# A recurrence and a mixer on one core: another order of the instructions, and transposes as pairs of 64-row blocks

## The chip, the core and the metric

The kernel runs on one core of a Trainium2 chip. A core has a tensor engine (TensorE, PE in the profile; its weight loads are listed as PEld), three engines for elementwise work (VectorE or DVE, ScalarE or ACT, GpSimd or POOL) and a queue engine (SyncE or SP) that issues transfers; sixteen DMA engines carry these. Each engine works through its own list of instructions in order and waits on semaphores for the others. The metric is the device time of one execution in microseconds (us).

## What is computed

Two stages follow each other, and the result is that of the second. The first is a recurrence over 768 time steps for 4 batches and 8 heads of 40 channels, with a state of 40x40 for each head:

```python
for t in range(S):
    y[:, :, t] = np.einsum('bhd,bhde->bhe', rt, state)
    Sa = np.einsum('bhde,bhe->bhd', state, at)
    state_decay = state * wt[:, :, None, :] - np.einsum('bhd,bhe->bhde', Sa, bt)
    state = state_decay + np.einsum('bhd,bhe->bhde', vt, kt)
```

The second takes y as x, with the 8 heads side by side as 320 channels:

```python
theta = x @ w_theta
yr = np.einsum('ts,bsd->btd', w_tok_r, x * np.cos(theta))
yi = np.einsum('ts,bsd->btd', w_tok_i, x * np.sin(theta))
u = x + (yr + yi)
return u + np.maximum(u @ w_ch, 0.0)
```

Inputs and output are float32; the kernel multiplies in bfloat16.

## The kernel before

The recurrence is worked off in 24 chunks of 128 time steps, 6 for each batch (`N = 24`, index `i`). For each chunk these steps follow; the names in quotes are the kinds by which the code calls its operations:

- Loads of w, k, b, a, v and r, 160 KB each, issued by SyncE (`load`, L409 and L421). The buffers are few (4 for w, 4 for k and b, 5 for a, 2 pairs for r), so a load waits until its buffer is free.
- Preparation (`prep`, L438 on): logarithm and cumulative sums of w (ACT and PE, "cs"), exponentials (ACT), products of k, b and a with them (POOL, L429: "kb", "ah"), casts of v and r (POOL or ACT, L435 and L434).
- Transposes on PE (`transpose_pairs`, L391; `turn_runs`, L538; `turn_back`, L557). A transpose is a matmul with the identity: the block of 128x128 is the stationary operand, the identity the moving one, and the result stands in PSUM, the accumulator memory of 8 banks. ACT (L394) or DVE (L397) then evacuates it to SBUF. "tkb" has 8 blocks, "ta", "tv" and "nut" 4 each, "tr" 8, "to" 8, "tb" 4.
- Scores (`scores`, L569): for the eight heads, eight matmuls of 64 rows and 128 columns ("spsi", "sphi", "slv", "slu"). Two heads lie in the upper and lower half of the rows and write to two different banks. A triangular mask follows, on DVE in one step (L578), or on ACT as a copy (L580) with a selection on POOL behind it (L582).
- The recurrence between chunks ("x0", "nu", "gt", "gd", L610 to L684) and the read-out ("y", L793 to L809).
- The mixer: x transposed ("xt", L711, 5 blocks for two chunks), times w_theta ("th", L763 and L773), copied (L828, "eth"), sine and cosine on ACT, products with x on POOL (L865, "z"); once a batch is complete, the mix over tokens ("row", L881: two times six matmuls of 320 columns for each output block), u transposed ("ut", L711), times w_ch ("ch", L763, L773), and the result stored (L920). The token weights come in through POOL's own queue (L960, "wdma") and are transposed ("wt", L968, 6 blocks).

All these operations are first collected in a list of 1602 with costs and dependences (`Plan.add`). Nothing is ordered at run time: `ORDER` (L26) is a written list of the 1602 numbers in which the operations are emitted, so it fixes the order on every engine. `HOMES` (L122) names the PSUM bank of each new PSUM tile in that order, and `PICK` (L138) names the operations that take the second of their two forms, such as a mask on ACT instead of DVE. PSUM is divided: banks 0 to 3 hold tiles of two banks (`doubles`, L355: only scores, and the token mix of the last two blocks), banks 4 to 7 tiles of one (`singles`, L356). Eleven transposes (`CROSSBAR`, L24) don't run on PE but as DMA transposes from SyncE's queue. `WARM` (L145) puts 49 matmuls on constant data into the start.

Of the kernel before, what the change touches and what calls it, by code (L numbers as in the profile page):

```python
# [144 lines left out]
WARM = {21: 25, 30: 4, 33: 1, 28: 8, 41: 11}  # L145


class Op:
# [53 lines left out]
def mm(n):  # L202
    return max(n / 2.4 + 2.5, 25.0)
# [853 lines left out]
```

## Time and profile before

| what | value |
|---|---|
| times of three runs | 197.72, 198.29 and 202.19 us; median 198.29 |
| span of the profiled execution | 197.8 us |
| instructions | 8019 |
| matmuls | 3288 |
| first input load issued | 0.8 us |
| last input load issued | 150.8 us |
| data moved | 32.75 MB, mean 166 GB/s |

The span runs from the first to the last instruction of the profiled execution; it stands 0.5 us under the median. An engine is busy from the start of an instruction to its end. Matmuls overlap each other, so PE's busy time says only when PE had something under way, and the distance between the starts of two matmuls says what one costs. In the rows of groups, "out<-in" names the tiles, the numbers behind the bar are the sum in us and the mean in ns, and the last part is idle time of the engine before these instructions with what ended it. SPq is SyncE's queue: the time that issuing a transfer took. The granted clock of TensorE is 1.00 in all stages.

### The profile page before, as it was taken

How to read it: one execution, taken by the hardware profiler on the slowest of the kernel's cores; microseconds unless marked ns; L12 is line 12 of the kernel's file. 1: busy time of each engine (PE TensorE's matmuls, PEld its weight loads, DVE VectorE, ACT ScalarE, POOL GpSimd, SP SyncE). 2: the span in 40 equal slices, each digit the busy share in tenths (PEclk: the TensorE clock that was granted, in tenths of full speed). 3: DMA queues.
4: the chain of work that ended last, by engine and by line, in shares of the span. 5: the costliest groups of instructions: out<-in, count | busy, mean ns of one | idle time of the engine just before them, and what ended most of it. 6: DMA issues, size and time to landing. Idle time of an engine off the chain costs nothing.

```text
span 197.8 us, 8019 instructions
## 1 busy us (share of the span) xinstructions
PE 187.6 (95%) x3288; PEld 150.3 (76%) x3288; DVE 164.3 (83%) x261; ACT 151.7 (77%) x337; POOL 145.1 (73%) x210
## 2 busy tenths in 40 slices
PE   7888999999989999999999999999999999999992
PEld 6776787777768788878878888888887878767661
DVE  5269899999989999888887988999999988675453
ACT  3584979799889988979988598888998986575111
POOL 8267544679879999699799939769699697558100
PEclk9999999999999999999999999999999999999999
DMA  6999879989999999999998899988998274863055
GB/s 119 210 212 163 154 161 196 182 166 197 233 174 173 207 171 185 190 185 223 153 210 168 153 187 170 188 148 169 182 155 163 43 177 102 87 194 104 0 191 174
DMA packets 134644, 32.75 MB, mean 166 GB/s; under 512 B 124816, under 2 KB 134608, under 8 KB 134608
## 3 DMA queue, kind: packets, MB, share of 16 engines
q1 hardware_dynamic: 131680, 29.19, 75.1%
q0 software_dynamic: 2784, 2.97, 9.6%
q8 instruction: 25, 0.41, 0.9%
q10 hardware_dynamic: 144, 0.08, 0.1%
q14 instruction: 11, 0.09, 0.1%
HBM read 29.54 MB, written 3.93 MB: 169 GB/s over the span
## 4 chain that ended last, share of the span: by engine, by line
PE 68%; DMA 9%; ACT 8%; SPq 6%; DVE 3%; issue 3%; POOL 1%; ACTq 0%; DVEq 0%; POOLq 0%
PE ps_s L881 17%; PE ps_s L391 10%; PE ps_d L569 9%; PE ps_s L763 5%; SPq L409 4%; DMA raw_w<-in_w_dram 3%; DMA raw_kb<-in_k_dram 3%; PE ps_s L711 3%; PE ps_s L652 2%; PE ps_s L629 2%; SPq L421 2%; DMA raw_r<-in_r_dram 2%; PE ps_s L538 2%; PE ps_s L773 2%; ACT cs L850 2%
## 5 line engine op out<-in xcount | busy, mean ns | idle before, releaser
L429 POOL TENSOR_TENSOR kb<-raw_kb,ex 128x320 bf16<-128x320 f32 x46 | 36.8, 811 | 9.7 <-DMA raw_kb<-in_k_dram 3.3
L881 PE MATMUL ps_s<-zr,wtok_r 128*128 128x320 bf16 x132 | 37.6, 299 | 0.0
L881 PE MATMUL ps_s<-zi,wtok_i 128*128 128x320 bf16 x132 | 37.5, 299 | 0.0
L578 DVE TENSOR_TENSOR lamu<-ps_d,mask_p 128x1024 bf16<-128x1024 f32 x22 | 26.8, 1219 | 1.7 <-PE ps_d L569 1.6
L578 DVE TENSOR_TENSOR psi<-ps_d,mask_p 128x1024 bf16<-128x1024 f32 x22 | 26.8, 1218 | 1.6 <-PE ps_d L569 1.4
L578 DVE TENSOR_TENSOR lamv<-ps_d,mask_p 128x1024 bf16<-128x1024 f32 x17 | 20.7, 1218 | 2.6 <-PE ps_d L569 1.8
L429 POOL TENSOR_TENSOR ah<-raw_a,we 128x320 bf16<-128x320 f32 x22 | 19.0, 866 | 3.6 <-DMA raw_a<-in_a_dram 1.6
L578 DVE TENSOR_TENSOR phi<-ps_d,mask_n 128x1024 bf16<-128x1024 f32 x17 | 20.7, 1218 | 0.9 <-PE ps_d L569 0.8
L865 POOL TENSOR_TENSOR zi<-cs,xp 128x320 bf16<-128x320 f32 x21 | 16.9, 816 | 3.3 <-ACT cs L850 3.3
L881 PEld LDWEIGHTS <-wtok_r 128*128 128x128 bf16 x144 | 14.0, 97 | 4.5
L569 PE MATMUL ps_d<-aT,kbT 64*128 64x128 bf16 x384 | 17.1, 217 | 0.2
L881 PEld LDWEIGHTS <-wtok_i 128*128 128x128 bf16 x144 | 14.1, 98 | 3.5
L391 PE MATMUL ps_s<-wide,kb 128*128 128x128 bf16 x184 | 15.0, 223 | 1.0 <-POOL kb L429 0.7
L865 POOL TENSOR_TENSOR zr<-cs,xp 128x320 bf16<-128x320 f32 x19 | 15.3, 810 | 0.7 <-ACT cs L850 0.7
L667 POOL TENSOR_TENSOR gt<-sum,ex 128x320 bf16<-128x320 f32 x13 | 9.5, 733 | 8.0 <-DVE sum L663 4.8
L800 PE MATMUL ps_s<-kb,lamv 128*128 128x40 bf16 x192 | 15.0, 180 | 0.0
L802 PE MATMUL ps_s<-kb,lamu 128*128 128x40 bf16 x192 | 14.9, 179 | 0.0
L569 PEld LDWEIGHTS <-kbT 64*128 64x128 bf16 x384 | 11.8, 94 | 3.1 <-ACT kbT L394 1.0
L800 PEld LDWEIGHTS <-lamv 128*128 128x128 bf16 x192 | 13.2, 96 | 0.6
L887 DVE TENSOR_TENSOR up<-ps_s,xp 128x320 bf16<-128x320 f32 x22 | 10.7, 488 | 3.5 <-PE ps_s L881 3.1
L435 POOL CAST r<-raw_r 128x640 bf16<-128x640 f32 x12 | 8.6, 720 | 6.5 <-DMA raw_r<-in_r_dram 6.5
L445 ACT ACTIVATE lw<-raw_w 128x320 bf16<-128x320 f32 x24 | 11.4, 475 | 2.6 <-DMA raw_w<-in_w_dram 2.6
(176 smaller groups left out, 606.7 us busy)
## 6 DMA issues: line engine op xcount, KB each, us to landing
raw_w<-in_w_dram SPq DMA_DIRECT2D x24, 160.0 KB, 4.1
raw_v<-in_v_dram SPq DMA_DIRECT2D x24, 160.0 KB, 3.9
raw_a<-in_a_dram SPq DMA_DIRECT2D x24, 160.0 KB, 4.2
raw_kb<-in_k_dram SPq DMA_DIRECT2D x24, 160.0 KB, 3.7
raw_kb<-in_b_dram SPq DMA_DIRECT2D x24, 160.0 KB, 4.0
raw_r<-in_r_dram SPq DMA_DIRECT2D x24, 160.0 KB, 4.4
out_dram<-oo SPq DMA_DIRECT2D x9, 160.0 KB, 2.0
wrow_i<-in_moe_w_tok_i_dram POOLq DMA_DIRECT2D x6, 192.0 KB, 5.3
```

The lines of the kernel that those rows point to most:

```text
L391: nc.tensor.transpose(out=dst[:, c:c + 128], in_=pair(src, g), identity=ident)
L429: pool = ("POOL", lambda: nc.gpsimd.tensor_tensor(out=dst, in0=in0, in1=in1, op=ALU.mult))
L445: add("ACT", "ln", i, lambda: nc.scalar.activation(out=paired(lw)[:, :, :, 0:D], in_=paired(raw_w[s4]), func=AF.Ln), 473, [("raw_w", s4)], ...
L569: nc.tensor.matmul(t[:, q, g, :], lhsT=lhs[g][rows(q)], rhs=rhs[g][rows(q)], start=True, stop=True)
L578: add("DVE", kindm, i, lambda: nc.vector.tensor_tensor(out=flat, in0=whole(), in1=mask.to_broadcast([128, 2 * G, 128]), op=ALU.mult), 1217 ...
L667: add("POOL", "wgt", i, lambda: nc.gpsimd.tensor_tensor(out=new_state, in0=sum_t, in1=wm.to_broadcast([128, 8, D]), op=ALU.mult), 830, [(" ...
L763: nc.tensor.matmul(ps(pk)[:, 0:DM], lhsT=lhs[:, 3 * c + kt, :], rhs=wt[:, 3 * c + kt, :], start=kt == 0, stop=kt == 2, skip_group_check=n ...
L800: nc.tensor.matmul(o, lhsT=lamv[:, p, g, :], rhs=kb[:, 0, h, 0:D], start=first, stop=False, skip_group_check=True)
L802: nc.tensor.matmul(o, lhsT=lamu[:, p, g, :], rhs=kb[:, 1, h, 0:D], start=False, stop=True, skip_group_check=True)
L865: pool = ("POOL", lambda: nc.gpsimd.tensor_tensor(out=dst, in0=in0, in1=in1, op=ALU.mult))
L881: nc.tensor.matmul(acc(), lhsT=wtok[nm][j][:, s], rhs=zs[c][:, s], start=n == 0 and c == 0, stop=n == NT - 1 and c == 1)
L887: add("DVE", "uadd", q, lambda: nc.vector.tensor_tensor(out=u, in0=acc(), in1=x, op=ALU.add), 488, [pk, x_key(q)], [u_key(q)], at="row")
```

## The change

The 1602 operations, their dependences and the inputs stay. Seven things change.

1. `ORDER` is another permutation. Up to about the first fifth the order on each engine is as before (the first 91 of PE's 596 operations, 70 of ACT's, 38 of DVE's, 24 of POOL's, 47 of SyncE's 180); behind that every engine has another order.
2. A transposing operation has a second form. In place of one matmul of 128 rows and 128 columns for a block it issues two of 64 rows and 64 columns, the upper half of the rows into one bank and the lower half into the next.
3. `PICK` names the operations in their other form: 94 before, 177 now. 54 of them are transposing operations that become pairs: 13 "tkb", 12 "nut", 8 "ut", 6 "tr", 5 "tv", 4 "xt", 4 "wt", 2 "ta". Together they have 308 of the 749 blocks that PE transposes (in 139 operations).
4. The evacuations read a pair's result from two banks (`src[:, :, ...]`), with the halves of 64 interleaved in the destination.
5. PSUM is one tile of eight banks, and any bank may hold any tile; a tile of two banks takes any two neighbours.
6. Some work moves between engines, by the other entries of `PICK`: masks on ACT and POOL 23 instead of 18 of 96; "eth" copies on DVE 9 instead of 1; evacuations "ea" on DVE 10 instead of 8, "ekb" 6 instead of 8, "enut" 5 instead of 7; "egd" copies on DVE 2 instead of 0, "nx" 4 instead of 2; casts of v on ACT 7 instead of 5, of r 3 instead of 0; products "z" on DVE 1 of the usual ones instead of 5, "kb" 2 more and "ah" 1 more on DVE.
7. `WARM`'s matmuls go to named banks 0 to 2 instead of the bank of the operation that they precede.

The list was planned with at most five of SyncE's transfers under way. The code holds nothing of this but the order.

Counted in the order of PE's operations, neighbours change between 128-row and 64-row work (scores, pairs, and the 64-row parts of "th" and "ch") 134 times before and 164 times now:

| up to PE's operation | stands at, before | changes before | changes now | blocks in pairs now |
|---|---|---|---|---|
| 142 | about 60 us | 48 | 49 | 33 |
| 441 | about 150 us | 107 | 133 | 248 |
| 596 | the end | 134 | 164 | 308 |

SyncE's transfers 48 to 56 are, before: r6, r6, b8, r8, w9, k8, r8, a8, w10 (the letter is the tensor, the number the chunk, r in two halves). Now: r8, r6, k8, r6, v10, b8, w9, r8, a8. The four token weight loads that POOL issues between 45.0 and 49.2 us are spread: counted by PE's work ahead of them, of which 26 us correspond to about 39 us of time and 42 to about 60, they stood together at 33 to 35 us and stand now at 26, 34, 39 and 39.

The diff, cut to its core (the lists are left out):

```diff
-PICK = [
+PICK = {
...
-WARM = {21: 25, 30: 4, 33: 1, 28: 8, 41: 11}
+WARM = {21: (0, 25), 30: (1, 4), 33: (2, 1), 28: (1, 8), 41: (1, 11)}
...
-        for n in PICK:
-            self.ops[n].eng, self.ops[n].fn = self.ops[n].alts[0]
+        for n, m in PICK.items():
+            o = self.ops[n]
+            o.eng, o.fn = o.alts[m - 1][:2]
+            if o.eng == "PE":
+                o.new = (o.new[0], 2)
...
-    doubles = [psum.tile([128, 2, 512], FP32, name=f"ps_d{i}") for i in range(DOUBLE // 2)]
-    singles = [psum.tile([128, 512], FP32, name=f"ps_s{i}") for i in range(BANKS - DOUBLE)]
+    banks = psum.tile([128, BANKS, 512], FP32, name="banks")
...
-        return doubles[h[0] // 2] if len(h) == 2 else singles[h[0] - DOUBLE]
+        return banks[:, h[0]:h[0] + 2] if len(h) == 2 else banks[:, h[0]]
+
+    def split(key):
+        return len(plan.home[key]) == 2
...
-    def transpose_pairs(dst, srcs):
-        for j, src in enumerate(srcs):
-            for g in range(G):
-                c = (j * G + g) * 128
-                nc.tensor.transpose(out=dst[:, c:c + 128], in_=pair(src, g), identity=ident)
...
+    def turned(kind, i, key, srcs, reads, cost, at="tile"):
+
+        def go():
+            if not split(key):
+                t = ps(key).bitcast(BF16)
+                for m, src in enumerate(srcs()):
+                    nc.tensor.transpose(out=t[:, m * 128:m * 128 + 128], in_=src, identity=ident)
+                return
+            for m, src in enumerate(srcs()):
+                for c in range(2):
+                    nc.tensor.transpose(out=ps(key)[:, c].bitcast(BF16)[:, m * 64:m * 64 + 64],
+                                        in_=src[rows(c)], identity=ident[rows(c), rows(c)])
+        add("PE", kind, i, go, cost, reads, [key], at=at, new=(key, 1), tail=tail(128),
+            alts=(("PE", go),))
...
+        def copy(op, out, dt, w):
+            one, src = n * w // 64, ps(psk) if w == 32 else ps(psk).bitcast(BF16)
+            if not split(psk):
+                at = (part or 0) * one
+                op(out=out, in_=src[:, at:at + one])
+            elif part is not None:
+                op(out=out, in_=src[:, part, 0:one])
+            else:
+                op(out=out.rearrange("p (n c w) -> p c n w", c=2, w=w),
+                   in_=src[:, :, 0:one // 2].rearrange("p c (n w) -> p c n w", w=w))
...
-            t = ps(o.new[0])
-            t = t[:, 0] if len(t.shape) == 3 else t
-            for _ in range(WARM[o.idx]):
-                nc.tensor.matmul(t[:, 0:128], lhsT=busy[:, 0:128], rhs=busy[:, 0:128],
+            at, n = WARM[o.idx]
+            for _ in range(n):
+                nc.tensor.matmul(banks[:, at, 0:128], lhsT=busy[:, 0:128], rhs=busy[:, 0:128],
                                  start=True, stop=True, skip_group_check=True)
```

More of the change, by code (lines that the diff above doesn't have):

```diff
@@ L508, in tr @@
             n = 4 * len(srcs)
[L509 to L510 removed]
+            turned(kind, i, p, lambda: pairs_of(srcs), skeys, n * mm(128))
             evac(eng, kinde, i, p, dst, n * 128, writes=[dkey])
@@ L531, in turn_runs, with tokens @@
         pr = ("ps", "t" + nm, i)
+        def tokens(t, q):
+            if nm == "r":
+                return t.rearrange("p (a t q g) -> p q t a g", a=2, q=8, g=2)[:, q]
+            return t.rearrange("p (t q g) -> p q t g", q=8, g=G)[:, q]
         def go():
[L534 removed]
             for q in range(8):
[L536 to L540 removed]
+                src = t[:, q].rearrange("p c d -> p (c d)")
+                if not split(pr):
+                    nc.tensor.transpose(out=tokens(ps(pr).bitcast(BF16), q), in_=src, identity=ident)
+                    continue
+                for c in range(2):
+                    nc.tensor.transpose(out=tokens(ps(pr)[:, c].bitcast(BF16)[:, 0:512], q),
+                                        in_=src[rows(c)], identity=ident[rows(c), rows(c)])
+        add("PE", "t" + nm, i, go, 8 * mm(128), [(nm, s)], [pr], new=(pr, 1), tail=tail(128),
+            alts=(("PE", go),))
         for x, (dst, dkey) in enumerate(dsts):
@@ L706, in feature_major @@
         n = len(blocks)
-        def go():
-            t = ps(p).bitcast(BF16)
-            for m, src in enumerate(blocks):
-                nc.tensor.transpose(out=t[:, m * 128:m * 128 + 128], in_=src, identity=ident)
-        add("PE", kind, q, go, n * mm(128), skeys, [p], at=at, new=(p, 1), tail=tail(128))
+        turned(kind, q, p, lambda: blocks, skeys, n * mm(128), at)
         evac("ACT", kinde, q, p, dst[:, 0:n, :].rearrange("p a b -> p (a b)"), n * 128,
@@ L963, in wtok_block @@
             p = ("ps", "wt" + nm, tb)
-            def go(row=row, p=p):
-                t = ps(p).bitcast(BF16)
-                for s in range(NT):
-                    nc.tensor.transpose(out=t[:, s * 128:(s + 1) * 128],
-                                        in_=row[:, s * 128:(s + 1) * 128], identity=ident)
-            add("PE", "wt", i, go, 6 * mm(128), [("wrow", nm, tb % 2)], [p], new=(p, 1),
-                tail=tail(128))
-            dst = wtok[nm][tb]
-            add("DVE", "ewt", i, lambda dst=dst, p=p: nc.vector.tensor_copy(
-                out=dst, in_=ps(p)[:, 0:384].bitcast(BF16).rearrange("p (a b) -> p a b", b=128)),
-                550, [p], [("wtok", nm, tb)], alts=(("ACT", lambda dst=dst, p=p: nc.scalar.copy(
-                    out=dst.bitcast(FP32),
-                    in_=ps(p)[:, 0:384].rearrange("p (a b) -> p a b", b=64))),))
+            turned("wt", i, p, lambda row=row: [row[:, s * 128:(s + 1) * 128] for s in range(NT)],
+                   [("wrow", nm, tb % 2)], 6 * mm(128))
+            evac("DVE", "ewt", i, p, wtok[nm][tb].rearrange("p a b -> p (a b)"), 768,
+                 [("wtok", nm, tb)])
     def mix_rows(bi):
```

44 lines of the change are left out of this document (15 added, 29 removed), and 242 rows, old and new, of tables (HOMES, ORDER, PICK).

## The prediction, made before the changed kernel ran

> **What bounds the kernel now.** I read the page's busy times and chain first, then the table by stage, then single matmuls in the timeline, and last the transfers of the stage before 60 us.
>
> ```profile
> span 197.8 us, 8019 instructions
> PE 187.6 (95%) x3288; PEld 150.3 (76%) x3288; DVE 164.3 (83%) x261; ACT 151.7 (77%) x337; POOL 145.1 (73%) x210
> ...
> q1 hardware_dynamic: 131680, 29.19, 75.1%
> q0 software_dynamic: 2784, 2.97, 9.6%
> ...
> PE 68%; DMA 9%; ACT 8%; SPq 6%; DVE 3%; issue 3%; POOL 1%; ACTq 0%; DVEq 0%; POOLq 0%
> ```
>
> TensorE (PE) is busy for 95% of the span and holds 68% of the chain that ended last. Those are averages, so the stages come next: time, then busy time of PE, weight loads, DVE, ACT and POOL, the granted clock, the DMA share and GB/s.
>
> ```profile
> 0.00:60.00 60.00, 54.13 (x993) 44.14 (x993) 49.43 (x85) 46.29 (x112) 40.72 (x72) 1.00 0.94 181
> 60.00:95.00 35.00, 34.91 (x672) 28.69 (x671) 31.82 (x45) 32.05 (x72) 32.94 (x48) 1.00 1.09 189
> 95.00:150.00 55.00, 54.55 (x1021) 44.99 (x1019) 49.75 (x75) 47.33 (x105) 45.85 (x62) 1.00 0.93 172
> 150.00:190.00 40.00, 40.00 (x581) 30.14 (x578) 29.62 (x51) 25.06 (x48) 25.57 (x31) 1.00 0.51 113
> ```
>
> Before 60 us PE idles for 5.9 us (60 - 54.13) while the DMA engines are 94% busy. From 60 to 190 us PE is busy for 129.5 of 130 us (34.91 + 54.55 + 40.00) at the full clock. So after 60 us whatever shortens PE's own work shortens the kernel, unless something close behind takes over: DMA at 1.09 from 60 to 95 us is the nearest, and it falls to 0.51 after 150 us.
>
> A busy PE here hides how many matmuls are in flight, so I price its work by the distance between starts:
>
> ```profile
> 81.26 0.49 PE L968 MATMUL ps_s<-wide,wrow_i 128*128 128x128 bf16 x6
> 81.59 0.50 PE L968 MATMUL ps_s<-wide,wrow_r 128*128 128x128 bf16 x6
> ...
> 82.77 0.50 PE L968 MATMUL ps_s<-wide,wrow_r 128*128 128x128 bf16 x6
> 83.20 0.40 PE L569 MATMUL ps_d<-aT,kbT 64*128 64x128 bf16 x8
> 83.43 0.39 PE L569 MATMUL ps_d<-rT,nuT 64*128 64x128 bf16 x8
> 83.76 0.62 PE L391 MATMUL ps_s<-wide,kb 128*128 128x128 bf16 x8
> ...
> 89.57 0.18 PE L800 MATMUL ps_s<-kb,lamv 128*128 128x40 bf16 x1
> 89.59 0.18 PE L802 MATMUL ps_s<-kb,lamu 128*128 128x40 bf16 x1
> 89.62 0.18 PE L800 MATMUL ps_s<-kb,lamv 128*128 128x40 bf16 x1
> 89.65 0.18 PE L802 MATMUL ps_s<-kb,lamu 128*128 128x40 bf16 x1
> ```
>
> Six whole transposes of 128 columns take 0.33 us (81.26 to 81.59): 55 ns each. Eight 64-row matmuls of 128 columns (scores) take 0.23 us (83.20 to 83.43), so two of them, one in each half of the rows, take 57 ns, hardly more than one whole matmul. Narrow matmuls of 40 columns start about 25 ns apart. And a change between 128-row and 64-row matmuls costs 0.10 us each way: the six transposes at 82.77 need 0.33 us, but the scores start 0.43 us later; the eight scores at 83.43 need 0.23 us, but the transposes start 0.33 us later.
>
> **The change part by part.**
>
> *Pairs instead of whole transposes.* The new list of choices turns 54 of PE's 139 transposing calls into pairs, with 308 of their 749 blocks. A whole block is one matmul of 128 rows and 128 columns; a pair is two of 64 rows and 64 columns, each in its own half of the rows and its own bank. No row here shows a 64-row matmul of 64 columns. Its lower bound is the distance at which any narrow matmul follows another, 25 ns for the pair if the halves run side by side; its upper bound is 50 ns, if each of the two needs that distance for itself. I take 29 ns, half of the scores' 57, because the score pair is the nearest row: it has the same 64-row loads and the same two halves, and only the columns differ. A block saves 55 - 29 = 26 ns, all blocks 308 x 26 = 8.0 us (9.2 to 1.5 at the bounds).
>
> The Trainium skill speaks against this edit: "TensorEngine Tiling (Array Packing)", section Instruction Overhead, says that a matmul has an overhead of about 60 cycles, that one of 1 column takes as long as one of 60, and that no tiling factor should be taken from a dimension that is already small. The 25 ns of the 40-column rows agree with that floor; whether it counts for both halves together no run here shows, since the scores, at 29 ns a matmul, stay above it. By that rule the pair costs 50 ns, and the case is worked out as the first rival.
>
> *More changes of row mode.* In PE's order the neighbours alternate between 128-row and 64-row work 134 times before and 164 times after, with the pairs counted as 64-row work: 30 more, at 0.10 us 3.0 us. Most pairs stand beside scores (52 of 54 have a 64-row neighbour), which is why 54 calls bring only 30 changes. The bounds are small here: the two distances above are 0.10 each.
>
> *Where these fall.* Ahead of 60 us stand 142 of PE's 596 operations. Among the first 142 of the new order lie 33 of the 308 blocks and one of the 30 additional changes: 0.9 us saved less 0.1. In that stage the loads end the waits (below), so I count it at nothing; if they did not, it would be 0.8 us. After 60 us: 275 blocks x 26 ns = 7.2 us, less 29 x 0.10 = 2.9 us, gives **-4.3 us**.
>
> *The new order of the transfers.* The first 47 of SyncE's 180 transfers keep their order. Behind them come the loads for chunks 6 to 9, and there nothing has slack:
>
> ```profile
> 45.81 0.54 SPq L409 DMA_DIRECT2D raw_kb<-in_b_dram  x1
> 46.44 1.57 SPq L421 DMA_DIRECT2D raw_r<-in_r_dram  x1
> 48.11 0.55 SPq L409 DMA_DIRECT2D raw_w<-in_w_dram  x1
> 48.70 1.37 SPq L409 DMA_DIRECT2D raw_kb<-in_k_dram  x1
> ...
> POOL kb L429 <- DMA raw_kb<-in_k_dram: 2.6, 2, 1.7
> ACT lw L445 <- DMA raw_w<-in_w_dram: 1.0, 1, 1.0
> ...
> 45.01 0.60 POOL L960 DMA_DIRECT2D wrow_i<-in_moe_w_tok_i_dram  x1
> ...
> 49.18 0.59 POOL L960 DMA_DIRECT2D wrow_r<-in_moe_w_tok_r_dram  x1
> ...
> DMA to landing us min/median/max: 2.7/4.0/8.8
> ...
> raw_w<-in_w_dram SPq DMA_DIRECT2D x24, 160.0 KB, 4.1
> ...
> wrow_i<-in_moe_w_tok_i_dram POOLq DMA_DIRECT2D x6, 192.0 KB, 5.3
> ```
>
> Between 40 and 60 us POOL and ACT wait for loads. In the new order chunk 8's b falls from the third place of this stretch to the sixth, behind the r of chunk 8 and the v of chunk 10: by the old issues from 45.81 to 48.70, 2.9 us later. Against that, four loads of token weights that POOL issues from 45.01 to 49.18 are spread: one goes before this stretch, two behind it. At the stage's 181 GB/s each (192 KB, 0.197 MB) is 1.1 us of all the DMA engines, and the two that go behind give back 2.2 us. Net **+0.7 us** (from -1.6, if PE's idle time of 40 to 60 us, 20 less the 9.58 and 8.80 of the rows below, goes, to +2.9, if the weights relieve nothing).
>
> ```profile
> 40.00:50.00 10.00, 9.58 (x191) 7.64 (x189) 9.98 (x14) 9.61 (x22) 8.71 (x13) 1.00 0.99 180
> 50.00:60.00 10.00, 8.80 (x186) 7.22 (x182) 8.88 (x11) 8.65 (x23) 8.13 (x11) 1.00 1.06 201
> ```
>
> "At most five under way" is a property of the plan; no wait is added for it. A load lands 4.0 us after its issue and the 144 input loads (six tensors, 24 each) leave in some 150 us, about one per us, so about four are under way already. Alone it is worth nothing.
>
> *Other engines.* The new choices move five more masks from DVE to ACT and POOL, eight more theta copies from ACT to DVE, casts from POOL to ACT and products between DVE and POOL.
>
> ```profile
> L578 DVE TENSOR_TENSOR phi<-ps_d,mask_n 128x1024 bf16<-128x1024 f32 x17 | 20.7, 1218 | 0.9 <-PE ps_d L569 0.8
> L828 ACT COPY th<-ps_s 128x320 f32<-128x320 f32 x22 | 8.6, 436 | 2.4 <-PE ps_s L773 1.3 <-PE ps_s L763 0.8
> ```
>
> A mask costs DVE 1.22 us and a theta copy costs ACT 0.44, so five of the one take 6.1 us off DVE and eight of the other 3.5 off ACT, and the rest goes the other way: each engine's total stays within about 3 us. From 60 to 190 us ACT has 25 us and DVE 19 us of idle time that cover this; POOL has 26 there but only 2.1 from 60 to 95, and if that cover failed its 3 us would be PE's. An evacuation of a pair reads as many elements as before, in two banks: taken as equal. A pair holds two banks for one; in the new order PE has enough work between the old content's matmuls and the new ones to cover the evacuation nearly everywhere after 60 us, so I add nothing.
>
> *Sum.* 197.8 - 4.3 + 0.7 = **194.2 us**. The span stands 0.5 us under the median of the three times (198.29; they run from 197.72 to 202.19), and I forecast on the scale of the span.
>
> **Rivals.**
>
> *A pair costs as much as its two matmuls one after the other* (50 ns). The 25 ns rows speak for it, the scores' 57 ns for two against it. After 60 us: 275 x 5 ns = 1.4 us saved, 2.9 us of mode changes paid, +0.7: 197.8 + 2.2 = **200.0 us**, slower than before. The point from which it decides: above 55 - 2900/275 = 44 ns a block the change loses PE time.
>
> *The loads become the bound until the last has landed* (about 150 us). For it: DMA 1.09 busy from 60 to 95 us and 0.93 to 150, the same bytes before and after, and a PE that wants them sooner. Against it: the DMA rate of that last stage is 172 GB/s, below the 189 shown just before, so there is room. Then only what lies after 150 us counts: 60 blocks x 26 = 1.6 us, less 4 changes, 0.4: 197.8 - 1.2 + 0.7 = **197.3 us**.
>
> *The new order also closes the gaps before 60 us*: the 1.6 us of idle PE between 40 and 60 us and the 0.8 us of pairs there go too, and the 0.7 is not paid: 197.8 - 4.3 - 1.6 - 0.8 = **191.1 us**.
>
> *All eight banks as one tile make waits coarser*, so that a matmul waits for evacuations of other banks. Each of the 96 masks of 1.2 us that stopped PE would show; even a tenth of them is 12 us: **210 us**. Nothing in the code asks for it, as every access names its banks.
>
> **How the numbers follow.** Forecast 0.56, expensive pairs 0.12, loads as the bound 0.17, gaps closed 0.11, coarse waits 0.04. The likeliest case's own range is 192.5 to 196.5. About 2% is what a measurement can tell from no change; 2% under the median is 194.3, which splits the forecast nearly in half (0.28 of its 0.56 below it), so faster is 0.28 + 0.11, with a little from the loads' case: 0.41. Slower by 2% means over 202.3: the coarse waits and the far end of expensive pairs, 0.07. Same: 0.52. The range goes from 191.0, the closed gaps, to 199.0, which takes in the loads' case and leaves out most of the expensive pairs and the coarse waits.
>
> **What would show it.** In the changed kernel's timeline a pair call of eight blocks should run in about 0.23 us of starts, against 0.44 for a whole one; 0.40 would mean the first rival. PE's matmuls should rise by 308 to about 3600, and mode changes of 0.10 us should stand around most pairs. PE should stay as busy from 60 us on; if instead POOL and ACT wait for raw tiles after 60 us, the loads bind. Chunk 8's b should land about a microsecond later than now. The forecast is wrong if pairs cost over 44 ns, if PE idles by more than 1 us after 60 us, or if the stage before 60 us moves by more than its bounds.

## The result, and the profile after

The changed kernel takes 199.96 us (median of 20 runs, 198.02 to 202.62), the kernel before on the same chip 198.74 us (median of 20, 196.82 to 204.86). The ratio is 1.0059, with a 95% interval from 1.0033 to 1.0084: slower by 0.6%, where 194.2 us was forecast. Here and below a ratio leaves out slow runs (over 1.5% above the fastest of their kernel) and a median takes in all, so a ratio need not be the quotient of two medians.

Time and span are not the same scale: the execution profiled below took 199.86 us and has a span of 198.1, and the distance is about 1.7 us in most executions of both kernels. So the profile before, with its span of 197.8, shows an execution of about 199.5 us (an estimate), 0.8 over the median of its kernel. The two spans differ by 0.3 us where the medians differ by 1.2.

First the head of the page of the changed kernel and its chain:

```profile
span 198.1 us, 8626 instructions
PE 183.0 (92%) x3596; PEld 143.1 (72%) x3596; DVE 164.0 (83%) x270; ACT 153.2 (77%) x333; POOL 148.2 (75%) x210
...
PE 66%; DVE 9%; DMA 6%; ACT 5%; POOL 4%; issue 3%; SPq 3%; ACTq 0%; DVEq 0%; POOLq 0%
```

PE's busy time fell from 187.6 to 183.0 us, by 4.6. The span did not fall, so PE is idle for 15.1 us (198.1 - 183.0) where it was idle for 10.2 (197.8 - 187.6): 4.9 us more. The table by stage, with the columns as in the prediction, tells where:

```profile
0.00:60.00 60.00, 51.69 (x1004) 42.56 (x1005) 48.40 (x88) 45.89 (x104) 41.45 (x72) 0.97 0.92 177
60.00:95.00 35.00, 34.06 (x732) 26.69 (x730) 30.71 (x47) 31.86 (x70) 33.89 (x47) 1.00 1.07 185
95.00:150.00 55.00, 54.92 (x1257) 44.09 (x1255) 51.52 (x82) 50.16 (x112) 48.19 (x64) 1.00 0.93 178
150.00:190.00 40.00, 38.97 (x594) 27.84 (x587) 30.33 (x49) 24.42 (x48) 24.65 (x30) 1.00 0.52 123
190.00:198.00 8.00, 3.37 (x32) 1.89 (x29) 3.02 (x8) 0.92 (x3) 0.00 (x0) 0.83 0.37 126
```

Idle time before 60 us rose from 5.9 to 8.3 us, from 60 to 150 us from 0.5 to 1.0, from 150 to 190 us from nothing to 1.0, and behind 190 us from 3.8 (7.8 less 4.0 of busy time) to 4.7 (8.1 - 3.4). The DMA share hardly moved in any stage. The granted clock was lower than before in two places, 0.97 before 60 us (0.91 in the first 20) and 0.83 behind 190; the waits named below come back in e5, whose clock is 1.00 up to 190 us, so the clock does not make them. Next, what PE waited for in the changed kernel (total, times, longest); first behind ScalarE between 40 and 60 us, then two rows of the whole span:

```profile
PE banks L607 <- ACT nuT L430: 0.7, 1, 0.7
PE banks L412 <- ACT vT L426: 0.6, 1, 0.6
PE banks L607 <- ACT rT L588: 0.5, 1, 0.5
PE banks L667 <- ACT nx L660: 0.4, 1, 0.4
```

```profile
PE banks L796 <- ACT uT L426: 1.0, 1, 1.0
...
PE banks L412 <- DVE kb L459: 0.8, 1, 0.8
```

The kernel before had 0.9 us behind ScalarE's nuT in that first stretch and 0.3 each behind r and kb. In the new order four waits of 0.4 to 0.7 us stand behind ScalarE's copies alone, 2.2 us together, and one of 0.7 behind GpSimd's ah. The two rows of the second fence lie at 194 and 160 us; the kernel before waited 0.3 us for its uT near the end, and for no kb behind 60 us.

The wait at 194 us is the simplest to read. ScalarE's list around it, with the DMA that ScalarE issues itself, and then PE's last matmuls:

```profile
192.01 0.32 ACT L430 COPY uT<-banks 128x192 f32<-128x192 f32 x1 [1.73 <-PE banks L412]
193.21 0.37 ACTq L942 DMA_DIRECT2D out_dram<-wrow_r  x1
193.63 0.32 ACT L426 COPY uT<-banks 128x192 f32<-128x192 f32 x1 [1.30 <-DVE wrow_r L938]
```

```profile
191.86 0.34 PE L408 MATMUL banks<-wide,us 128*128 128x128 bf16 x3
192.38 0.59 PE L785 MATMUL banks<-wch,uT 128*128 128x160 bf16 x6 [0.19 <-ACT uT L430]
194.00 0.58 PE L796 MATMUL banks<-wch,uT 128*128 128x320 bf16 x3 [1.03 <-ACT uT L426]
```

The transposition that feeds the last evacuation started at 191.86 us. The evacuation (eut 22) could have followed the first one at about 192.3, but in the new list a store of an output row stands ahead of it on ScalarE, and that store waits for VectorE's row. So the copy starts at 193.63 and PE's last mixing at 194.00. In the old list the evacuation stands ahead of the store.

The pairs, on the other hand, did what was forecast. Two places of PE's timeline where a pair call is followed by other 64-row work:

```profile
80.52 0.34 PE L412 MATMUL banks<-wide,wrow_r 64*128 64x64 bf16 x12
80.70 0.40 PE L412 MATMUL banks<-wide,kb 64*128 64x64 bf16 x16
...
88.24 0.41 PE L412 MATMUL banks<-wide,kb 64*128 64x64 bf16 x16
88.48 0.28 PE L412 MATMUL banks<-wide,nu 64*128 64x64 bf16 x8
```

Six blocks take 0.18 us (80.52 to 80.70) and eight take 0.24 (88.24 to 88.48): 30 ns a block, where 29 was taken and 55 is a whole one.

### The profile page after: what moved, and what is told of

The parts are those of the page before. It is cut to its first block, busy times and chain, and to the rows that moved or that the text cites. A ratio compares the mean times of both kernels' runs of the same rounds, so it can differ in the third digit from the quotient of the medians.

```text
span 198.1 us, 8626 instructions
## 1 busy us (share of the span) xinstructions
PE 183.0 (92%) x3596; PEld 143.1 (72%) x3596; DVE 164.0 (83%) x270; ACT 153.2 (77%) x333; POOL 148.2 (75%) x210
## 4 chain that ended last, share of the span: by engine, by line
PE 66%; DVE 9%; DMA 6%; ACT 5%; POOL 4%; issue 3%; SPq 3%; ACTq 0%; DVEq 0%; POOLq 0%
PE banks L914 17%; PE banks L607 11%; PE banks L408 9%; PE banks L796 5%; PE banks L412 4%; DMA raw_a<-in_a_dram 3%; PE banks L690 2%; PE banks L667 2%; PE banks L573 2%; DMA raw_v<-in_v_dram 2%; DMA out_dram<-o 2%; PE banks L806 2%; PE banks L654 2%; PE banks L648 2%; PE banks L835 2%
## 5 line engine op out<-in xcount | busy, mean ns | idle before, releaser
L914 PE MATMUL banks<-zr,wtok_r 128*128 128x320 bf16 x144 | 41.2, 300 | 0.6 <-POOL zr L898 0.5
L914 PE MATMUL banks<-zi,wtok_i 128*128 128x320 bf16 x144 | 41.0, 299 | 0.0
L616 DVE TENSOR_TENSOR lamu<-banks,mask_p 128x1024 bf16<-128x1024 f32 x23 | 28.1, 1220 | 2.9 <-PE banks L607 2.3
L616 DVE TENSOR_TENSOR psi<-banks,mask_p 128x1024 bf16<-128x1024 f32 x23 | 28.0, 1218 | 2.2 <-PE banks L607 2.2
L607 PE MATMUL banks<-aT,kbT 64*128 64x128 bf16 x384 | 17.9, 221 | 0.4 <-ACT kbT L426 0.2
L616 DVE TENSOR_TENSOR phi<-banks,mask_n 128x1024 bf16<-128x1024 f32 x14 | 17.0, 1217 | 1.5 <-POOL r L466 1.3
L616 DVE TENSOR_TENSOR lamv<-banks,mask_p 128x1024 bf16<-128x1024 f32 x13 | 15.8, 1219 | 1.4 <-PE banks L607 1.2
L833 PE MATMUL banks<-kb,lamv 128*128 128x40 bf16 x192 | 14.8, 180 | 0.0
L835 PE MATMUL banks<-kb,lamu 128*128 128x40 bf16 x192 | 14.7, 179 | 0.0
L835 PEld LDWEIGHTS <-lamu 128*128 128x128 bf16 x192 | 13.0, 96 | 0.1
```

The costliest lines, as they stand in the source:

```text
L607: nc.tensor.matmul(t[:, q, g, :], lhsT=lhs[g][rows(q)], rhs=rhs[g][rows(q)], start=True, stop=True)
L616: add("DVE", kindm, i, lambda: nc.vector.tensor_tensor(out=flat, in0=whole(), in1=mask.to_broadcast([128, 2 * G, 128]), op=ALU.mult), 1217 ...
L833: nc.tensor.matmul(o, lhsT=lamv[:, p, g, :], rhs=kb[:, 0, h, 0:D], start=first, stop=False, skip_group_check=True)
L835: nc.tensor.matmul(o, lhsT=lamu[:, p, g, :], rhs=kb[:, 1, h, 0:D], start=False, stop=True, skip_group_check=True)
L914: nc.tensor.matmul(acc(), lhsT=wtok[nm][j][:, s], rhs=zs[c][:, s], start=n == 0 and c == 0, stop=n == NT - 1 and c == 1)
```

## The experiments

Each ratio stands against runs of the kernel before that were taken together with it (their medians are 198.71 to 199.10 us); the medians of the kernels stand beside. "Short transfers" means that from chunk 6 on each load leaves out half of its rows, so the outputs differ.

| kernel | median, us | ratio | interval |
|---|---|---|---|
| the change | 199.96 | 1.0059 | 1.0033 to 1.0084 |
| e1 new order, no pairs | 204.86 | 1.0299 | 1.0257 to 1.0341 |
| e2 change, eut 22 earlier | 199.65 | 0.9967 | 0.9918 to 1.0016 |
| e3 old to 70 us, then new | 202.52 | 1.0049 | 0.9994 to 1.0104 |
| e4 new to 61 us, then old | 208.73 | 1.0446 | 1.0382 to 1.0509 |
| e5 change, short transfers | 199.04 | 0.9993 | 0.9965 to 1.0020 |
| e6 before, short transfers | 197.36 | 0.9927 | 0.9892 to 0.9962 |
| e7 old order, new code | 199.24 | 1.0010 | 0.9973 to 1.0046 |
| e8 old order with pairs | 203.41 | 1.0189 | 1.0127 to 1.0251 |
| e9 change, two mends | 199.01 | 1.0007 | 0.9964 to 1.0049 |
| e10 all lists reworked | 217.16 | 1.0880 | 1.0829 to 1.0931 |
| e11 old to 73 us, then new, mends | 200.91 | 1.0111 | 1.0070 to 1.0151 |
| e12 as e11, short transfers | 197.89 | 0.9943 | 0.9914 to 0.9972 |
| e13 as e11, joined at 86 us | 200.55 | 1.0033 | 0.9993 to 1.0072 |
| e14 as e12, transposes' queue | 199.57 | 0.9986 | 0.9938 to 1.0035 |
| e15 change, four mends | 202.41 | 1.0056 | 0.9991 to 1.0121 |
| e16 change, eut 22, short | 197.68 | 0.9918 | 0.9891 to 0.9945 |
| e17 as e16, kb 22 first | 198.36 | 0.9977 | 0.9944 to 1.0011 |
| e18 as e16, products on GpSimd | 198.28 | 0.9992 | 0.9953 to 1.0030 |

My first theory was: the pairs work, and waits in the new lists of the other engines give the time back. The rivals: the pairs cost elsewhere what they save on PE, the transfers became the bound, or one tile for all banks makes waits coarser.

**e1, order without pairs.** The 54 entries of the list of choices that turn a transposition into a pair are left out; nothing else.

```diff
 PICK = {
-    286: 1, 336: 1, 370: 1, 391: 1,
...
 }
```

> The new order, banks and engines, but all 54 paired transpositions whole again (308 blocks). Theory: the pairs work as forecast, and what took the gain back is TensorE's idle time in other places; then PE's work grows by 308 x 26 ns = 8.0 us, less two mode changes of 0.10 us, and since PE is busy for over nine tenths of the span most of it shows: 204 to 208 us, 1.027 to 1.047 of the kernel before. Rival 1: the pairs themselves cost what they save (44 ns a block or more in place, or by their evacuations): 198 to 200.5 us, 0.995 to 1.01. Rival 2: the new order is bound by transfers or by the other engines whatever PE does: 200 to 202 us, 1.006 to 1.015.

It came out at 204.86 us, as the theory had it. Its page:

```profile
span 204.2 us, 8006 instructions
PE 190.6 (93%) x3288; PEld 149.9 (73%) x3288; DVE 165.8 (81%) x270; ACT 154.5 (76%) x333; POOL 147.9 (72%) x210
```

This splits the change in two. The order alone (before to e1) adds 3.0 us of PE's busy time (190.6 - 187.6; 28 more mode changes at 0.10 are 2.8; e7, with the work of the kernel before, has 188.2, so such a difference is good to about 0.6) and 3.4 us of idle time (13.6 - 10.2). The pairs alone (e1 to the change) take off 7.6 us of busy time (forecast for all blocks: 8.0) and add 1.5 us of idle time (15.1 - 13.6). So in the new order the pairs are worth 6.1 us of span and 4.9 of the medians. The order costs somewhat more: 6.1 us of the medians.

**e7, the old order in the new code.** Order, banks, engine choices and warm-up matmuls are those of before, in the changed code.

```diff
-ORDER, HOMES, PICK, WARM of the change
+ORDER, HOMES, PICK, WARM of the kernel before, no pairs
```

> The changed code with the old order, banks, engine choices and no pairs: what is left of the change is that the eight banks are one tile and that transpositions and evacuations go through the new helpers. Theory: this costs nothing, 198.2 to 199.2 us, 0.997 to 1.003. Rival: one tile for all banks makes waits coarser: 200 us and above, over 1.006.

At 1.0010 it can't be told from the kernel before. No cost of one tile for all banks and of the new helpers shows; the interval leaves room for 0.5%.

**e5 and e6, short transfers in both kernels.**

```diff
         for key, dst, src in load(i):
+            if i >= 6:
+                dst, src = dst[0:64], src[0:64]
             add("SP", "l" + key[0][4:], i,
...
-                    out=to[:, c], in_=runs[c])
+                    out=to[0:64 if i >= 6 else 128, c], in_=runs[c][0:16 if i >= 6 else 32])
```

> The changed kernel with shorter transfers: from chunk 6 on each load of r, k, v, w, a and b fills only half of its rows, the other half keeps an older chunk's numbers, so the outputs differ; instructions, order, banks and waits stay. Theory: pairs took work off PE until the 16 transfer engines, nine tenths busy up to 150 us, had nothing in hand, and late transfers at the heads of GpSimd's and ScalarE's lists give the gain back; then this falls by 4 to 7 us, to 193 to 196 us, 0.97 to 0.985 of the kernel before, and by more than the same cut in the kernel before. Rival: the idle time is made on the chip (banks, evacuations, the order of the other engines): 198 to 200 us, 0.997 to 1.006.

> The kernel before with the same shorter transfers from chunk 6 on (half of each load's rows keep older numbers, so the outputs differ). Theory: its PE has 5 us more to do, so that transfers hold it less: 196 to 198 us, 0.985 to 0.997; the changed kernel with short transfers is then 1 to 4 us faster than this. Rival: both fall by the same, or neither, and the changed kernel stays about 1 us slower.

Here the theory that I had by then, that late transfers eat the gain, fell. From 60 to 150 us the short transfers leave the DMA engines busy for 0.63 of the time, where the two stages above had 1.07 and 0.93; this row is the changed kernel's:

```profile
60.00:150.00 90.00, 89.53 (x2005) 71.44 (x2001) 83.03 (x129) 82.59 (x183) 82.23 (x110) 1.00 0.63 106
```

Yet the changed kernel gains 0.7% by it (1.0059 to 0.9993) and the kernel before as much (to 0.9927). The transfers cost both about 1.4 us, and the difference between the two stays. PE's longest waits behind ScalarE between 40 and 60 us stay too, with the same lengths, and so does the one at the end:

```profile
PE banks L609 <- ACT nuT L430: 0.7, 1, 0.7
PE banks L412 <- ACT vT L426: 0.6, 1, 0.6
...
PE banks L798 <- ACT uT L426: 1.0, 1, 1.0
```

They recur in another execution, and late transfers from chunk 6 on don't make them. The stage before 60 us shows this best, first in e6, then in e5, both at the full clock:

```profile
0.00:60.00 60.00, 56.30 (x1059) 46.37 (x1061) 51.35 (x88) 48.54 (x117) 43.94 (x77) 1.00 0.87 159
0.00:60.00 60.00, 53.00 (x1021) 43.53 (x1021) 48.87 (x89) 46.65 (x107) 42.52 (x74) 1.00 0.82 150
```

With the old order PE is idle there for 3.7 us, with the new one for 7.0; between 20 and 60 us it is 0.6 against 3.4. Behind 60 us it is 4.3 against 6.3. So the larger part of the added idle time lies before 60 us. The short transfers also take away scatter here: the ten runs of e5 lie within 1.7 us, the 20 of the change within 4.6. That does not hold for each kernel with short transfers: e14, e17 and e18 scatter by 4.6, 3.4 and 2.6 us.

**e2 and e16, the last wait.** The evacuation moves ahead of the store, first with whole, later with short transfers.

```diff
-    1595, 1573, 1549, 1551, 1574, 1582, 1596, 1597, 1571, 1572, 1598, 1600, 1599, 1601, 1583,
+    1595, 1573, 1549, 1551, 1574, 1582, 1583, 1596, 1597, 1571, 1572, 1598, 1600, 1599, 1601,
```

> The changed kernel with one instruction moved: ScalarE's evacuation eut 22 stands directly behind the transposition ut 22, ahead of the last-but-one output row and its store on ScalarE's own queue. Theory: the store, which waits for the row, holds the evacuation and with it PE's last mixing by 1.0 to 1.2 us; then the time falls by 0.8 to 1.2 us, to 0.999 to 1.003 of the kernel before. Rival: the last output rows on VectorE and their stores set the end anyway: no change, 1.004 to 1.008.

> The changed kernel with short transfers (half of each load's rows from chunk 6 on keep older numbers, so the outputs differ), and eut 22 directly behind ut 22. With short transfers the runs lie within 0.6 us, so that single waits can be priced. Theory: the wait of 1.20 us for eut 22 is all at the end: 199.04 less 0.9 to 1.2, so 197.8 to 198.1 us, 0.993 to 0.996 of the kernel before. Rival (something else sets the end): 198.8 to 199.2 us.

With whole transfers the ratio falls from 1.0059 to 0.9967, but the runs scatter from 196.81 to 204.03 and the median falls by 0.3 us only, so e16 repeats it with short ones: from 199.04 (e5) to 197.68 us, or 1.4 us, and the two intervals lie apart. PE's last two rows in e2 follow without a wait for uT of chunk 22:

```profile
196.15 0.59 PE L781 MATMUL banks<-wch,uT 128*128 128x160 bf16 x6 [0.19 <-ACT uT L426]
196.57 0.57 PE L792 MATMUL banks<-wch,uT 128*128 128x320 bf16 x3
```

One store's place in ScalarE's list is worth more than the whole measured difference (1.2 us). Nothing stands behind this wait (1.0 us in the trace), and it comes back in full. But with this wait gone and the transfers short, the changed kernel (e16, 0.9918) only draws level with the kernel before (e6, 0.9927): the work that the pairs save still does not show.

**e9, e17 and e18, the wait at 160 us.** The change moved three products, kb 22, kb 23 and ah 23, from GpSimd to VectorE, and on VectorE kb 22 stands behind both of chunk 23's. e9 is e2 with kb 22 back on GpSimd. e17 is e16 with kb 22 ahead of the other two on VectorE. e18 is e16 with all three on GpSimd, kb 22 early.

```diff
 e9:   PICK   -  1412: 1
 e17:  ORDER  -  ... 1472, 1474, ..., 1412     +  ... 1412, 1472, 1474
 e18:  PICK   -  1412: 1, 1472: 1, 1474: 1     ORDER  +  1412 behind 1473
```

> The changed kernel with two instructions set back: eut 22 directly behind ut 22 on ScalarE (as in the run with the moved evacuation), and the product kb 22 on GpSimd again, where the kernel before has it, and not behind six others on VectorE. No transfer, bank or pair is touched. Theory: the loss is made by single waits in the new lists of the other engines, the same in each execution: PE waits 1.20 us for eut 22 and 0.85 us for kb 22, so 2 us come back: 197.5 to 198.2 us where the changed kernel has 199.96, 0.994 to 0.998 of the kernel before. Rival: PE's idle time moves on to the next late operand, and under half of it comes back: 199 us and above, 1.001 or more.

> As the run before, and on VectorE chunk 22's product kb ahead of chunk 23's kb and ah instead of behind them. Theory: PE's wait of 0.85 us for kb 22 at 160 us goes and nothing follows it closely: another 0.6 to 0.9 us less, 197.0 to 197.4 us, 0.989 to 0.992. Rival, a lock between VectorE and GpSimd: the product stands beside GpSimd's run of products there and takes 2 to 5 us in place of 0.5, so the wait stays or grows: 198 us and above.

> As the first run of these three, with the three products that the change moved from GpSimd to VectorE (kb 22, kb 23, ah 23) back on GpSimd, kb 22 directly behind the other product of chunk 23. VectorE's list gets 2.8 us shorter there, GpSimd's 2.4 us longer. Theory (waits in lists): kb 22 is there 5 us earlier, but GpSimd's last products z 17 come 0.8 to 2.4 us later and PE waits for these at 158 us: 197.6 to 198.4 us, no gain. Rival (the engine choice was the fault): 197.0 to 197.3 us.

Both mends together should have brought 2 us. e9 brought back 1 (199.01), no more than e2 did alone (1.0007 against 0.9967; the intervals overlap). Among PE's waits the row of kb is gone, but a product of the mixer that GpSimd now makes later stands in its place:

```profile
PE banks L909 <- POOL zi L893: 1.1, 1, 1.1
```

e17 and e18 are no faster than e16 (198.36 and 198.28 against 197.68). PE's waits from 150 us on, in e16, e17 and e18:

```profile
PE banks L408 <- DVE kb L457: 0.8, 1, 0.8
PE banks L404 <- DVE o L948: 0.5, 1, 0.5
```

```profile
PE banks L794 <- DVE o L948: 1.4, 1, 1.4
PE banks L794 <- DMA xT<-xp: 0.8, 1, 0.8
```

```profile
PE banks L911 <- POOL zi L895: 1.4, 1, 1.4
PE banks L403 <- DVE o L947: 0.9, 1, 0.9
```

In e17 and e18 the wait for kb is traded for waits on what comes next: an output row on VectorE (in e17 VectorE waited 2.4 us for its buffer, until an earlier store had landed), a transposition by DMA, or GpSimd's mixer products. The rival of e17, a lock that stretches the product to 2 us or more, did not come about, though its time of 198 us and above did: the two kb took 2.0 us together. These waits in the middle of the kernel had another close behind them.

**e3, e4, e11, e12, e13, one order joined to the other.** e3 takes the first 541 operations in the old order and the rest in the new; e4 is the reverse with 459. e11 joins at 578 with the mends of e2 and e17, e12 is e11 with short transfers, e13 joins at 694.

```diff
-ORDER of the change
+ORDER = [first N of one order] + [the rest in the other], banks and engines likewise
```

> The first 541 operations in the old order with their old banks and engines (PE reaches their end at about 70 us), all the rest in the new order with its pairs. Theory: the new order loses 2.7 us of PE time before 70 us by waits for loads, ScalarE and GpSimd, and gains after it, so the old beginning with the new rest is 2 to 3 us faster than the changed kernel: 197 to 198 us, 0.990 to 0.997 of the kernel before. Rival: the loss lies behind 70 us, or is spread over the whole span: 199.5 to 201 us, 1.004 to 1.011.

> The other half: the first 459 operations in the new order with their new banks, engines and pairs (PE reaches their end at about 61 us), all the rest in the old order, with whole transpositions. Theory: the beginning is what lost, so that this is 1.5 to 3 us slower than the kernel before: 200.2 to 201.7 us, 1.008 to 1.015. Rival: the beginning costs nothing (loads bind there in both): 198.3 to 199.5 us, 0.998 to 1.004.

> The first 578 operations in the old order with their old banks and engines (PE reaches their end at about 73 us), the rest in the new order with its pairs (47 pairs, 271 blocks, 162 mode changes), eut 22 directly behind ut 22, and on VectorE chunk 22's product kb ahead of chunk 23's products. All transfers whole. PE's work is 271 x 26 ns less 28 x 0.095 us = 4.4 us under that of the kernel before. Theory of two bounds: the waits in the new lists before 73 us and at the two late places are gone, but PE then runs 3 to 4 us ahead into transfers that are not there yet, which give most of it back in some executions: 197 to 199.5 us, 0.99 to 1.003, with a wide spread. Rival, the lists alone: 194 to 195.5 us, 0.977 to 0.985. Rival, the other engines' work sets the pace whatever the lists: 199 to 200.5 us.

> The same joined kernel with short transfers from chunk 6 on (half of each load's rows keep older numbers, so the outputs differ), so that neither the new lists' waits nor late transfers are there. Theory of two bounds: only now the work that the pairs save shows: 193 to 195 us, 0.97 to 0.982, against 197.4 us for the kernel before with short transfers. Rival (the other engines' work sets the pace): 196.5 to 199 us.

> As the joined kernel with whole transfers, but joined at the 694th operation, which PE reaches at about 86 us (39 pairs, 224 blocks, 154 mode changes; PE's work 224 x 26 ns less 20 x 0.095 us = 3.9 us under that of the kernel before). PE gets ahead later, when fewer transfers are still to come. Theory of two bounds: 196 to 198.5 us, 0.986 to 0.998. Rival, the lists alone: 194.5 to 196 us. Rival, the other engines' work: 199 to 200.5 us.

With whole transfers none beat the kernel before, and e12 does not beat e6. A join also joins SyncE's list, and in e3 and e4 an engine then waits for a load near the seam, and PE behind it for 2.9 and 5.8 us. GpSimd's wait in e3, and ScalarE's in e4:

```profile
POOL v L459 <- DMA raw_v<-in_v_dram: 3.1, 1, 3.1
```

```profile
ACT lw L467 <- DMA raw_w<-in_w_dram: 7.9, 3, 5.8
```

In e13 PE's longest wait, 2.7 us, is for a transposition by DMA behind 150 us. So e3, e4 and e13 don't tell what the new beginning costs by itself: inconclusive. e11 against e12 does show that in a joined kernel the transfers cost 3.0 us (200.91 to 197.89), about twice what they cost in either original. And e12, with 4.4 us less PE work than e6 (4.1 of busy time, 183.0 against 187.1) and neither late transfers nor the early waits, is no faster than e6 (0.9943 against 0.9927, the intervals overlap); I had expected 193 to 195. Its PE waits behind 60 us:

```profile
PE banks L791 <- DMA xT<-xp: 1.4, 1, 1.4
PE banks L602 <- DMA aT<-ah: 1.0, 1, 1.0
PE banks L405 <- DMA wrow_r<-in_moe_w_tok_r_dram: 0.7, 1, 0.7
```

The first two are transpositions that SyncE's queue makes by DMA between 156 and 175 us, the third is a load of weights. e6 has no such wait: behind 60 us its longest is 0.3 us. The new beginning can be compared between e17 and e12, which have the same mends and the same short transfers. Between 20 and 60 us PE is idle for 3.4 us in e17 and for 0.6 in e12, but the times are 198.36 and 197.89 and the intervals overlap: of 2.8 us at most 0.5 comes through, and the rest goes into waits behind it.

**e14 and e15, that queue.** Chunk 23's kb and ah go to GpSimd early, their two transpositions to the head of the queue, ut 12 ahead of nut 22; in e14 on top of e12, in e15 on top of e2.

```diff
 PICK   -  1472: 1, 1474: 1
 ORDER  +  1472, 1474 behind 1473, then tkb 23 and ta 23; ut 12 behind tv 22
```

> The joined kernel with short transfers (half of each load's rows from chunk 6 on keep older numbers, so the outputs differ) and one more change: chunk 23's products kb and ah go from VectorE to GpSimd directly behind its other product of that chunk, and the two transpositions of that chunk that SyncE's queue makes by DMA stand ahead of the others there, ut 12 ahead of nut 22. Theory: with lists and transfers out of the way, PE waits on SyncE's queue of DMA transpositions (1.0 us for aT of chunk 23 and 1.4 us for xT of chunk 20); the first of the waits goes and part of the second: 195.8 to 197 us, 0.984 to 0.990, against 197.9 us without this change. Rival: this queue only looks late, and the time stays at 197.5 to 198.3 us.

> The changed kernel, all transfers whole, with four mends in its lists: eut 22 directly behind ut 22; on VectorE chunk 23's products kb and ah no longer ahead of chunk 22's kb, but on GpSimd behind that chunk's other product; SyncE's two transpositions of chunk 23 first, ut 12 ahead of nut 22. Theory: the three waits after 150 us (1.20 us for eut 22, 0.85 for kb 22, and the queue's) go and no list is longer in their place: 197.3 to 198.5 us, 0.991 to 0.998 of the kernel before, about 2 us under the changed kernel. Rival (waits move on, as with two mends): 198.7 to 199.6 us, 1.0 to 1.004.

Neither got faster: 0.9986 against 0.9943 for e12, and 1.0056 against 0.9967 for e2. The intervals overlap in both, though the medians are 1.7 and 2.8 us higher. Whether this queue is a bound of its own stays open, because my edit made a new wait: chunk 22's product on VectorE took 4.71 us (4.31 in e15), and PE waited 2.4 us for it in both. VectorE and GpSimd at that time in e14:

```profile
154.50 4.71 DVE L454 TENSOR_TENSOR kb<-raw_kb,ex 128x320 bf16<-128x320 f32 x1
159.13 0.48 DVE L837 TENSOR_TENSOR xp<-banks,we 128x320 bf16<-128x320 f32 x1
```

```profile
153.91 1.56 POOL L893 TENSOR_TENSOR zr<-cs,xp 128x320 bf16<-128x320 f32 x2
155.41 0.81 POOL L893 TENSOR_TENSOR zi<-cs,xp 128x320 bf16<-128x320 f32 x1
...
158.05 0.81 POOL L893 TENSOR_TENSOR zi<-cs,xp 128x320 bf16<-128x320 f32 x1
```

**e8 and e10, other combinations.** e8 puts 34 pairs (183 blocks) into the old order, with other banks for most operations. e10 moves operations in all five lists of the change, against the waits named above and by the durations of its trace.

```diff
 e8:   old ORDER; PICK + 34 transpositions as pairs; 384 of 430 HOMES other
 e10:  ORDER: 99 PE, 57 ACT, 18 DVE, 70 POOL, 96 SP operations moved; 67 HOMES, 33 engines other
```

> The old order and engine choices, with 34 of the transpositions (183 blocks, after 36 us) as pairs where two adjoining banks are free at that time in the trace of the kernel before, and other banks for most operations; 152 mode changes instead of 134. PE's work falls by 183 x 26 ns less 18 x 0.095 us = 3.0 us. If the new order is what costs and transfers hold the old one little: 195.5 to 197 us, 0.984 to 0.992. If transfers hold the old order as soon as PE has less to do: 197.5 to 199.5 us, 0.994 to 1.004, with a wide spread between runs.

> The changed kernel's lists reworked so that PE's named waits for other engines and for banks go: 99 of PE's 596 operations, 57 of ScalarE's, 18 of VectorE's, 70 of GpSimd's and 96 of SyncE's queue stand elsewhere in their lists, 67 of 430 bank choices and 33 engine choices are other, and 54 pairs with 321 blocks and 172 mode changes (the changed kernel: 54, 308 and 164). Theory: with the waits of the lists gone, the 7 us of PE work that pairs save show: 192.5 to 195 us, 0.97 to 0.982 of the kernel before. Rival: what holds PE back is the sum of the other engines' work or the transfers, and other lists only move the waits: 197.5 to 200 us, 0.994 to 1.006.

Both failed. e8 was to have 3.0 us less PE work than e7; its trace shows 1.0 less of busy time (187.2 against 188.2), and it is 4.2 us slower. As most of its banks differ too, it does not price pairs in the old order by themselves. PE waits 2.2 us for a transposition by DMA alone:

```profile
PE banks L788 <- DMA uT<-up: 2.2, 1, 2.2
```

e10 is the slowest of all: with SyncE's list moved as well, GpSimd and ScalarE wait 5.8 and 4.8 us for r and w. Several lists moved at once there, so it doesn't tell which one costs the time.

## Why the forecast was wrong, point by point

- **Pairs at 29 ns a block: right.** 30 ns by the starts, 7.6 us of PE's busy time for all 308 blocks (8.0 forecast). The first rival, 50 ns, is out; that its 200.0 us lies next to the measured 199.96 is chance. By the rule of the Trainium skill, "TensorEngine Tiling (Array Packing)", section Instruction Overhead, as I had read it, the two halves would have taken 50 ns; the trace does not agree, since with 30 ns for the pair the two halves don't pay the floor one after the other.
- **Mode changes at 0.10 us: in accord with e1**, which has 28 more than before and 3.0 us more busy time.
- **Eight banks as one tile: no cost that shows, as forecast** (e7, 1.0010).
- **Other engines' totals: right** within 3.1 us, but the wrong thing to look at. What e16 shows to count is the place of a single instruction in its list.
- **The stage before 60 us, +0.7: one of the two steps that failed.** I priced this stage by its loads alone ("in that stage the loads end the waits") and put the new lists of the other engines there at nothing. PE's idle time in it grew by 2.4 us, and by 3.3 where the transfers are short in both kernels (e6 to e5). In the changed kernel it stands mainly behind ScalarE's evacuations. Chunk 8's b, on which the +0.7 rested, is issued 1.3 us later (45.81 to 47.14), and no row of PE's waits names it. That 2.4 lies inside the stated bounds is luck, since the cause was another. No edit shows what this idle time is worth at the end; e17 against e12 lets 0.5 us of it through.
- **"So I add nothing" behind 60 us: the other.** The forecast let PE be as busy after 60 us as before and named 1 us of idle time as its limit. From 60 to 190 us PE was idle for 2.0 us where it had been for 0.5, and behind 190 us for 4.7 where it had been for 3.8. I argued from each engine's total of idle time and from PE's having other work; I did not look at what stands ahead of a given evacuation in ScalarE's list, though the new order shows it. Shown by an edit: the store ahead of eut 22 costs 1.4 us (e16). The 0.8 us behind kb 22 is a wait in the trace, but no edit of mine gained from removing it.
- **Loads as the bound, 197.3: not the cause** of the difference (e5, e6), although they cost each of the two kernels about 1.4 us.

The sum then reads: PE's busy time -4.6 (forecast -4.3 - 0.8), idle time +4.9 (forecast +0.7), span +0.3. What stays open is whether any order turns these 4.6 us into time, and with it the rival that the work of the other engines sets the pace whatever their lists: no run here takes work off them. Each kernel here that has 3 to 5 us less PE work than the one before (the change, e3, e8 and e11 to e15, by the count of pairs and mode changes) has a wait of 1 to 3 us that it has not, and not the same one: an evacuation, a load, a transposition by DMA, a product. The best with whole transfers, e2, can't be told from the kernel before (0.9967, up to 1.0016).

## What to carry to other kernels

When PE is 95% busy and the others 73 to 83%, work taken off PE is not yet time: list for each engine in order what now stands ahead of the operand that PE wants next, and price that before the saving. Look at the last few microseconds first, above all for a store that waits on an in-order engine ahead of an evacuation, since nothing behind it takes the time back; of 2.8 us of idle time before 60 us at most 0.5 came through to the end. And split such a change (order alone, pairs alone) before explaining it: the two parts here were +6 and -5 us.

## What the hardware showed

A product on VectorE with both operands in SBUF took 0.48 us at 13.18 us of the changed kernel, where GpSimd ran none. Beside GpSimd's products the three moved ones took 0.67 to 1.08 us, and GpSimd's took 1.04 or 1.05 where e14's stand at 0.81; in e14, beside six (and one cast) that followed each other without a gap, one took 4.71 us and ended 0.35 us after the last of them.

```profile
13.18 0.48 DVE L459 TENSOR_TENSOR kb<-raw_kb,ex 128x320 bf16<-128x320 f32 x1
...
157.04 1.03 DVE L459 TENSOR_TENSOR kb<-raw_kb,ex 128x320 bf16<-128x320 f32 x1
157.99 1.08 DVE L459 TENSOR_TENSOR ah<-raw_a,we 128x320 bf16<-128x320 f32 x1
```

```profile
157.67 1.05 POOL L898 TENSOR_TENSOR zi<-cs,xp 128x320 bf16<-128x320 f32 x1
158.68 1.04 POOL L898 TENSOR_TENSOR zr<-cs,xp 128x320 bf16<-128x320 f32 x1
```

The Trainium skill, "SBUF — State Buffer", section Who interferes with whom, says that VectorE and GpSimd share one pair of ports under an exclusive lock, and that a VectorE operation with two SBUF inputs takes part in it. The rows agree: both sides take longer when they meet. That a product on VectorE can end only behind a row of six on GpSimd is what these runs add (4.71 us in e14, 4.31 in e15).
